# A two-layer attention and Fourier kernel on one core: a table of leans for the order of the queues, constant products in TensorE's planned gaps, and places held for the last two block groups

## The chip, the cores and the metric

The kernel runs on one core of one Trainium2 chip. The metric is device time in microseconds (us); lower is better. TensorE is called PE in the profile (its weight loads PEld), VectorE DVE, ScalarE ACT, GpSimd POOL, and SyncE SP; SP issues the DMAs.

## The reference

The input x is 2048 rows by 512. Two kinds of layer alternate, twice each; every one adds its result to x, and every one begins with a normalization of the rows.

```python
def _A_ref(x, wq, wk, wv, wo, beta):        # attention with a memory
    H = 32; Dh = D // H; N = 4; L = S // N  # 32 heads of 16, 4 segments of 512 rows
    ...
    for s in range(N):
        qs, ks, vs = q[:, :, s], k[:, :, s], v[:, :, s]
        logits = jnp.einsum("bhqd,bhkd->bhqk", qs, ks) * scale + mask
        p = _softmax(logits, axis=-1)
        a_dot = jnp.einsum("bhqk,bhkd->bhqd", p, vs)
        pq = phi(qs)
        ...                                 # a_mem = phi(q) M / (phi(q) z)
        o = g * a_mem + (1.0 - g) * a_dot
        outs.append(o)
        pk = phi(ks)
        M = M + jnp.einsum("bhld,bhle->bhde", pk, vs)
        z = z + jnp.einsum("bhld->bhd", pk)
    ...
    return o @ wo

def _B_ref(x, ...):                         # Fourier mixing, the real part
    a = jnp.einsum("bsd,ed->bse", x, dft_hid_re)
    b = jnp.einsum("bsd,ed->bse", x, dft_hid_im)
    y = jnp.einsum("ts,bse->bte", dft_seq_re, a) - jnp.einsum("ts,bse->bte", dft_seq_im, b)
    return y

x = x + _A_ref(_layernorm(x), ...)
x = x + _B_ref(_layernorm(x), ...)
x = x + _A_ref(_layernorm(x), ...)
x = x + _B_ref(_layernorm(x), ...)
```

## The kernel before

**Tiling.** The program treats an attention and a Fourier part together as one layer, so it has two. The 2048 rows are 16 row tiles of 128, four to a segment. The 32 heads are four groups of eight. Layers, segments and groups together make 32 rounds. Most large products are made in float16 with each operand split into a high and a low half; three products (high by high, high by low, low by high) are summed.

**The work of a round.** The four row tiles of a segment are loaded and normalized (`t_ln`, line 554: statistics on DVE, a power on POOL, two activations on ACT, the low half on DVE or POOL, then a transposing DMA into the tile `g`). PE makes queries and keys (`s_p`), then values (`s_v`; ACT evicts them in `t_v`, line 703). The scores are made twice: once by rows, to get each row's maximum on DVE (`s_x`, `t_max`), and once transposed (`s_st`, line 889) for the exponentials on ACT and the causal mask on POOL (`t_sel`). The masked exponentials multiply the values (`s_av`, line 912), four heads beside each other in 32 columns of the array each. The result is merged with the memory part (`s_mem`, `s_m`).

**The Fourier part.** When a segment's four groups are done, `s_o` (line 971) makes the output projection, adds x, normalizes again, and `s_ab` multiplies by the transform along the row (512). The transform along the 2048 rows is split by block groups of row tiles: `CHUNKS = [2] * 6 + [4]`, six groups of two and a last one of four. For each group and each of 16 output tiles, `s_f` (line 1120) adds the group's share; these are the long runs of `w,w` products, 3072 in all. Their results are added to `y` (`t_y`, line 1106), and with the last group `t_y` writes the finished tile. The sequence matrix comes from memory in pieces of 256 KB (`s_r`, line 1018): in layer 0 raw, to be scaled and split by `s_c` and `t_c` (a maximum on DVE, one product with ones on PE, two activations on ACT, a subtraction) and stored; in layer 1 the stored halves are read back.

**Who sets the order.** Each engine works through its instructions in the order in which the program writes them. A planner (class `Plan`, line 47) sets that order while the program is written. Every kind of work is a Python generator: a stream (`s_...`, listed in line 1154) or a task that a stream starts (`t_...`). A generator yields what its next step needs: an engine, the tiles that it reads, the places that it takes. For every candidate `Plan.ready` and the free times of the engines give the time at which the step could start, and the earliest is written next (lines 1199 and 1200):

```python
best = min(ready, key=lambda q: (q[0] - LEAN.get(q[1][2] + q[1][0][0][0], 0),
                                 PRIO.get(q[1][2] + q[1][0][0][0], 5)))
```

The key of the table `LEAN` is the generator's name and the letter of the engine (T for TensorE, V, A, G for GpSimd, Y for SyncE): `t_yY` is the write of a finished `y` tile. A positive lean makes a step look earlier by that many ns. In this kernel the table is empty (line 32).

The attention-by-value products alternate between two units, each at half of the product's cost `c` (line 159).

**Places.** One pool `w` of 50 places (`NW`, line 25) holds most working tiles. Each kind has a floor and a ceiling: `slots_free` (line 88) refuses a place that would leave another kind short of its floor. `ab` is the kind of the inputs of the transform along the rows; its ceiling is 12, and `s_f` sets its floor when it comes to a block group (lines 1126 and 1127): 12 at the last but one (two tiles of two halves and four more tiles), 8 at the last, 4 at the others. The tile kind `dft` stands for a place in the accumulator memory.

Of the kernel before, what the change touches and what calls it, by code (L numbers as in the profile page):

```python
# [1 line left out]

# [24 lines left out]
CHUNKS = [2] * 6 + [4]  # L27
# [1 line left out]
BF16 = mybir.dt.bfloat16  # L29
NEG = -1e30  # L30
TICK = 10240 / 3
LEAN = {}
APART = dict(pj=(1, 4), av=(1, 2), dft=(0, 2), sx=(2, 4), st=(2, 4), ss=(0, 4))
SHARED = dict(pj=(1, 4), av=(0, 2), dft=(1, 2), sx=(0, 2), st=(0, 2), ss=(2, 6))
HOLD, SWITCH = 700.0, 95.0
# [3 lines left out]
BATCH = 4  # L39
AFTER = 4  # L40
PRIO = {}
DEEP = 1500.0
AHEAD = 2
NR = 2
# [2 lines left out]
class Plan:  # L47
# [4 lines left out]
    def __init__(self):  # L52
        self.free = dict.fromkeys("VGATYD", 0.0)
        self.acc = {}
        self.cols = {}
        self.wr = {}
        self.rd = {}
        self.area, self.count, self.slot = {}, {}, {}
        self.fresh = set()
        self.fine = {}  # L60
        self.by = {}
        self.dma = None
        self.lands = []
        self.ports = []
        self.mode, self.units, self.begun, self.entered = "m", {}, 0.0, 0.0

    def turn(self, mode):

# [75 lines left out]
    def op(self, eng, name, args, kw):  # L144
        aps = [a for a in list(args) + list(kw.values()) if isinstance(a, bass.AP)]
        out, ins = [aps[0]], aps[1:]
        if name == "tensor_tensor_reduce":
            out.append(ins.pop())
        n = max(a.free_size() for a in aps)
        lat = self.LAT[eng]  # L150
        src = any(a.space == bass.MemoryType.PSUM for a in ins)
        if eng == "T":
            n, w = out[0].free_size(), aps[1]
            slow = 4 if w.dtype == F32 else 1
            c = max(n / 2.4 * slow, (380 if n < 32 else 200) if slow > 1 else 55) + (18 if w.dtype == F32R else 3)
            cols = n * slow * w.partition_size() / 128
            mode, unit = "m", 0
            if name == "matmul" and out[0].partition_size() == 32:
                mode, unit, c = "v", out[0].start_partition() // 32 % 2, c / 2
            elif w.partition_size() <= 64:  # L160
                mode, unit = "h", w.start_partition() // 64
                if slow > 1:
                    unit, c = 0, c / 2
        elif eng == "A":
            c = n / 1.2 + (52 if src else 93) + (93 if any(a.free_size() == 1 for a in ins) else 0)
        elif eng == "V":
            c = 68 + n / 0.96
            if name == "reciprocal":
                c = 68 + n * 6.25
            elif name == "scalar_tensor_tensor" and out[0].dtype == F32:  # L170
                c += 60
            elif name == "tensor_copy" and out[0].dtype == F16:
                c = 68 + n / 1.92
            elif name == "tensor_scalar" and out[0].dtype == F32:
                c = 68 + n / (0.87 if src else 1.32)
        elif eng == "G":
            c = 127 + n * 0.915 if name == "affine_select" else 96 + n * 2.1
            if name == "tensor_tensor" and kw.get("op") == OP.pow:
                c = 300 + n * 165
            elif name == "partition_all_reduce":  # L180
                c = 370
        else:
            stored = out[0].space == bass.MemoryType.DRAM
            c, took, tail = self.dma or ((415, 917, 364) if stored else (470, 829, 755))
            took *= out[0].nbytes() / 262144 if self.dma is None else 1
            if kw.get("transpose"):
                c, took, tail = 1325, 850, 300
        t = self.free[eng]
        for a in ins:
            t = max(t, self.wr.get(self.key(a), 0.0))  # L190
        for o in out:
            m = self.key(o)
            t = max(t, self.rd.get(m, 0.0))
            if eng == "V" and "reduce" not in name or self.by.get(m, eng) != eng:
                t = max(t, self.wr.get(m, 0.0))
        psum = [self.key(a) for a in aps if a.space == bass.MemoryType.PSUM]
        for m in psum:
            for o, u in self.acc.get(m, {}).items():
                if o != eng:
                    t = max(t, u)  # L200
        if eng == "V" and name in SHAREPORT and not src:
            for b, e in self.ports[-8:]:
                if b <= t < e:
                    t = e
        if eng == "Y" and len(self.lands) >= 8:
            t = max(t, self.lands[-8])
        if eng == "T":
            if mode == self.mode:
                t = max(t, self.begun + 7, self.units.get(unit, 0.0))
            else:  # L210
                t = max(t, max(self.units.values(), default=0.0) + SWITCH)
                self.mode, self.units, self.entered = mode, {}, t
            k = int(t / TICK)
            if self.cols.get(k - 1, 0) < 3060:
                c = min(2 * c, max(c, (k + 1) * TICK - t + c / 2))
            self.cols[int((t + c) / TICK)] = self.cols.get(int((t + c) / TICK), 0) + cols
        e = t + c
        self.free[eng] = e
        if eng == "G" and name == "tensor_tensor":
            self.ports.append((t, e))  # L220
        if eng == "T":
            self.begun = t
            self.units[unit] = e
            if len(self.units) < dict(m=1, h=2, v=2)[mode]:
                self.free[eng] = t + 7
            else:
                self.free[eng] = min(self.units.values())
        if eng == "Y":
            self.free["D"] = max(self.free["D"], e + 590) + took
            e = self.free["D"] + tail  # L230
            self.lands.append(e)
        e += lat
        for m in psum:
            self.acc.setdefault(m, {})[eng] = e
        for a in ins:
            m = self.key(a)
            self.rd[m] = max(e, self.rd.get(m, 0.0))
        for o in out:
            m = self.key(o)
            self.wr[m] = e  # L240
            self.by[m] = eng
            self.fresh.discard(m)
        for a in ins + out:
            if a.tensor.name in self.slot:
                ar, b = self.slot[a.tensor.name]
                ar["last"][b] = max(ar["last"][b], e)
# [18 lines left out]
def body(ctx: ExitStack, tc: tile.TileContext, x, wq, wk, wv, wo, beta, wd, cs, out):  # L265
    nc = tc.nc
    pl = Plan()
# [852 lines left out]
    def s_f():  # L1120
        u = 0
        held, left = {}, {}
        for j, t in units:
            layer, r = chunks[j]
            if j not in held:
                low = 2 * sum(len(chunks[j + k][1]) for k in range(2) if j % len(CHUNKS) + k == last - 1 + k)
                pl.area["ab"]["kinds"]["ab"] = low or 2 * max(len(c[1]) for c in chunks[j:j + 2]), 12
                keys = [(layer, gt, e) for gt in r for e in range(2)]
                yield gate(*[("ab", *k) for k in keys])
                held[j], left[j] = [abs_.pop(k) for k in keys], NT  # L1130
            ab = held[j]
            n = len(r) // 2
            yield gate(*[("c", u + i) for i in range(n)])
            cc = prep[u:u + n]
            u += n
            yield need("T", *cc, *ab, tag="dft")
            p = ps("dft")
            for k in range(4 * n):
                c, b = cc[k // 4], ab[k]
                sl = slice(128 * (k % 4), 128 * (k % 4) + 128)  # L1140
                for i, (x, z) in enumerate(((0, 0), (0, 1), (1, 0))):
                    T.matmul(p, c[:, x, sl], b[:, z], start=(k == 0 and i == 0), stop=(k == 4 * n - 1 and i == 2))
                if k % 4 == 3:
                    pl.close(c)
                if k < 4 * n - 1:
                    yield need("T")
            f = place[j % len(CHUNKS), t]
            spawn(t_y(p, layer, t, fyu[:, f:f + 1], j % len(CHUNKS) == last))
            left[j] -= 1
            if not left[j]:  # L1150
                pl.close(*ab)
            yield need("T")
# [2 lines left out]
        s_ld, s_r, s_c, s_m, s_av, s_st, s_o, s_ln, s_w, s_x, s_mem, s_v, s_p, s_ab, s_f, s_wo, s_k)]  # L1155
    for s in streams:
        s[0] = next(s[1])
    def settle(s):
        while callable(s[0]) and s[0]():
            s[0] = next(s[1], None)  # L1160
        return s[0] is not None and not callable(s[0])

    while streams or tasks:
# [37 lines left out]
        if best is None:  # L1201
            assert not streams and not tasks, "stuck"
            break
        best[1][0] = next(best[1][1], None)

# [43 lines left out]
```

## Time and profile before

| | |
|---|---|
| Median of 3 runs | 1746.74 us (1741.66 to 1747.06) |
| The profiled execution, its own time | 1747.35 us |
| Its span, first to last instruction | 1745.6 us |
| Instructions | 32094, of which 10998 matmuls |
| Busy: PE, DVE, ACT, POOL | 1674.4, 1094.4, 870.9, 746.2 us |
| Mean granted TensorE clock | 0.971 |
| DMA | 225.00 MB, all working transfers on SP's queue |

All instructions go through one helper, line 258, so groups are told apart by tile names and not by lines: `b` is a place in the accumulator memory, `w` one of the 50 places, `g` the transposed normalized rows, `x` and `y` the rows of x between layers and the running sum of the transform. "out<-in" names what an instruction writes and reads. A stage is a stretch of the span; a busy time is given in us of that stretch. The granted clock of a stretch is a mean over its time: 1.00 is full speed.

### The profile page before, as it was taken

What the parts mean: (1) busy time and instruction counts of PE and PEld (TensorE: products, weight loads), DVE (VectorE), ACT (ScalarE), POOL (GpSimd) and SP (SyncE); (2) the same over time, 40 slices, a digit from 0 to 9 for tenths busy, and PEclk for the clock granted to TensorE, in tenths of its full rate; (3) what the DMA queues carried; (4) which work ended last, traced back from release to release, by engine and by line L of the source; (5) the groups of instructions that cost most, each with busy time, mean ns of one, the idle gap of its engine ahead of it and who ended that gap; (6) DMA issues with size and microseconds to landing.
All of it is one profiled execution on the core that took longest, in us unless ns stands there. A gap on an engine that the chain in (4) does not pass through costs nothing.

```text
span 1745.6 us, 32094 instructions
## 1 busy us (share of the span) xinstructions
PE 1674.4 (96%) x10998; PEld 730.6 (42%) x10998; DVE 1094.4 (63%) x3525; ACT 870.9 (50%) x1481; POOL 746.2 (43%) x1284
## 2 busy tenths in 40 slices
PE   6888899998999999999999999999999999999999
PEld 3333344443344443444535344443444443344444
DVE  7885856787675967654578676566675856443221
ACT  5597467555548365644366755464446334412000
POOL 4466355555546264633244644444535334312000
PEclk9788999999999999999989999999999999999999
DMA  8537445554247443334845654354444342131423
GB/s 194 165 102 205 109 113 156 150 145 128 77 125 212 139 130 107 108 105 135 223 139 189 188 164 121 74 138 132 113 120 122 94 110 85 56 121 23 136 85 118
DMA packets 217076, 225.00 MB, mean 129 GB/s; under 512 B 112968, under 2 KB 135496, under 8 KB 216912
## 3 DMA queue, kind: packets, MB, share of 16 engines
q1 hardware_dynamic: 216912, 222.95, 45.6%
q8 instruction: 86, 1.41, 0.3%
q14 instruction: 78, 0.64, 0.1%
HBM read 137.40 MB, written 61.87 MB: 114 GB/s over the span
## 4 chain that ended last, share of the span: by engine, by line
PE 80%; DVE 7%; issue 4%; DMA 3%; ACT 3%; POOL 2%; SPq 1%; DVEq 0%; POOLq 0%; ACTq 0%
PE b L258 80%; DVE junk L258 3%; ACT w L258 3%; POOL w L258 2%; DMA w<-w 1%; SPq L258 1%; DVE w L258 1%; DVE y L258 1%; DVE mx L258 1%; DMA x<-y 0%; DMA w<-in_x_dram 0%; DMA y<-in_wv_dram 0%; DVE bst L258 0%; DMA w<-x 0%; DVE cgm L258 0%
## 5 line engine op out<-in xcount | busy, mean ns | idle before, releaser
L258 PEld LDWEIGHTS <-w 128*128 128x128 f16 x4992 | 466.2, 98 | 636.9 <-issue 121.5
L258 PE MATMUL b<-w,w 128*128 128x512 f16 x3072 | 709.9, 381 | 4.2 <-POOL w L258 1.4
L258 ACT ACTIVATE w<-b,fac 128x512 f32<-128x512 f32 (+1 forms) x728 | 417.6, 653 | 196.1 <-PE b L258 191.8
L258 DVE CUSTOM_DVE_ANT_0 junk<-b,cmask 128x128 bf16<-128x128 f32 (+3 forms) x1024 | 437.1, 485 | 70.9 <-PE b L258 70.1
L258 POOL TENSOR_TENSOR w<-w,w 128x512 f16<-128x512 f32 (+1 forms) x260 | 309.2, 1193 | 239.1 <-ACT w L258 204.7
L258 POOL TENSOR_SCALAR_AFFINE_SELECT w<-w 128x128 f32<-128x128 f32 (+2 forms) x704 | 236.7, 348 | 272.6 <-ACT w L258 268.1
L258 DVE SCALAR_TENSOR_TENSOR y<-b,fyu,y 128x512 f32<-128x512 f32 x200 | 149.1, 745 | 210.7 <-PE b L258 209.8
L258 PE MATMUL b<-g,w 128*128 128x512 f16 x768 | 191.1, 394 | 6.7 <-POOL w L258 3.0
L258 ACT ACTIVATE w<-w,csc 128x512 f16<-128x512 f32 (+1 forms) x256 | 179.5, 721 | 25.2 <-DVE csc L258 20.3
L258 PE MATMUL b<-w,vt 128*32 128x512 f32 (+3 forms) x2048 | 181.5, 469 | 6.9 <-POOL w L258 4.7
L258 PE MATMUL b<-wd,w 128*128 128x512 f16 x768 | 182.1, 385 | 4.6 <-DMA w<-w 4.3
L258 ACT ACTIVATE w<-b 128x512 f16<-128x512 f32 x128 | 76.4, 599 | 218.0 <-PE b L258 210.6
L258 DVE SCALAR_TENSOR_TENSOR w<-b,w 128x512 f16<-128x512 f32 x128 | 87.9, 688 | 150.2 <-ACT w L258 149.2
L258 PE MATMUL b<-kst,qst 48*128 48x128 f16 (+3 forms) x1024 | 125.0, 309 | 10.9 <-DVE mx L258 5.0
L258 PE MATMUL b<-qst,kst 50*128 50x512 f16 (+3 forms) x1024 | 119.5, 308 | 10.4 <-DVE mx L258 3.8
L258 ACT ACTIVATE w<-w 128x512 f16<-128x512 f32 (+1 forms) x144 | 90.6, 632 | 58.1 <-DVE w L258 55.9
L258 PEld LDWEIGHTS b<-w,vt 128*32 128x32 f32 x2048 | 56.7, 113 | 95.8 <-issue 52.2
L258 PE MATMUL b<-w,g 128*128 128x128 f16 x1536 | 94.4, 219 | 0.4 <-ACT w L258 0.2
L258 PEld LDWEIGHTS <-g 128*128 128x128 f16 x1536 | 87.8, 98 | 13.9 <-issue 9.1
L258 DVE STREAM_TRANSPOSE w<-b 128x512 f32<-128x512 f32 x112 | 76.4, 699 | 22.1 <-PE b L258 13.7
L258 PE MATMUL b<-wo,w 128*128 128x512 f16 x384 | 89.3, 381 | 0.0
L258 PEld LDWEIGHTS <-kst 50*128 50x128 f16 x1024 | 37.5, 95 | 120.8 <-issue 109.5
(99 smaller groups left out, 1017.8 us busy)
## 6 DMA issues: line engine op xcount, KB each, us to landing
w<-in_cs_dram SPq DMA_DIRECT2D x128, 256.0 KB, 3.6
cc<-w SPq DMA_DIRECT2D x128, 256.0 KB, 2.5
w<-cc SPq DMA_DIRECT2D x128, 256.0 KB, 3.3
w<-w SPq DMA_DIRECT2D x96, 256.0 KB, 3.2
d<-w SPq DMA_DIRECT2D x128, 128.0 KB, 2.5
w<-in_x_dram SPq DMA_DIRECT2D x32, 256.0 KB, 3.2
qst<-d SPq DMA_DIRECT2D x64, 128.0 KB, 3.2
kst<-d SPq DMA_DIRECT2D x64, 128.0 KB, 2.8
```

The source lines that it names most:

```text
L258: r = f(*args, **kw)
```

## The change

It has four parts.

1. **Leans.** The table `LEAN` gets eight entries: transposed scores on PE 150 ns earlier, loads of the sequence matrix 600 ns earlier, the activations of the first normalization 1500 ns earlier, writes of `y` 2000 ns later, loads of x for the output projection 300 ns earlier, the scaling work of the sequence matrix 150 ns later, loads of x for the first normalization 1000 ns later, evictions of values 1000 ns earlier.
2. **Constant products.** `Plan` also records PE's work as (begin, end, columns); `lately(t)` is the number of columns worked in the 3413 ns before t. Ahead of each step on PE that the planner writes, `t_warm` looks at the planned gap. If the mask constant exists ("CM"), the gap less 300 ns is at least 500 ns, fewer than 4200 columns were worked lately, and an accumulator place of the kind `dft` is free by then, it writes products of the constant `onesb` by itself, 512 columns each, until the gap is full or 4200 columns are reached. Nothing reads the result.
3. **Cost of attention by value.** The planner's cost on a unit goes from `c / 2` to `c / 2 + 12` ns.
4. **Places.** The floor of `ab` is 12 at the last two block groups of a layer; before, it was 12 at the last but one and 8 at the last.

```diff
-LEAN = {}
+LEAN = dict(s_stT=150.0, s_rY=600.0, t_lnA=1500.0, t_yY=-2000.0, s_oY=300.0, s_cV=-150.0, s_lnY=-1000.0, t_vA=1000.0)
...
+WARM, IDLE, SPARE = 4200, 500.0, 300.0
...
+    def lately(self, t):
+
+        return sum(c * max(0.0, min(e, t) - max(b, t - TICK)) / (e - b) for b, e, c in self.work)
...
-                mode, unit, c = "v", out[0].start_partition() // 32 % 2, c / 2
+                mode, unit, c = "v", out[0].start_partition() // 32 % 2, c / 2 + 12
...
+            self.work.append((t, t + c, cols))
+            while self.work[0][1] < t - 3 * TICK:
+                self.work.popleft()
...
-                low = 2 * sum(len(chunks[j + k][1]) for k in range(2) if j % len(CHUNKS) + k == last - 1 + k)
-                pl.area["ab"]["kinds"]["ab"] = low or 2 * max(len(c[1]) for c in chunks[j:j + 2]), 12
+                low = 2 * max(len(c[1]) for c in chunks[j:j + 2])
+                if j % len(CHUNKS) >= last - 1:
+                    low = 2 * sum(CHUNKS[last - 1:])
+                pl.area["ab"]["kinds"]["ab"] = low, 12
...
+    def t_warm(at):
+        at -= SPARE
+        if "CM" not in done or at - pl.free["T"] < IDLE or pl.lately(at) >= WARM:
+            return
+        r = pl.slots_free(("dft",))
+        if r is None or r > at - IDLE:
+            return
+        old = {b: (pl.area["dft"]["last"][b], pl.area["dft"]["kind"].get(b)) for b in range(8)}
+        p = ps("dft")
+        ar, b = pl.slot[p.tensor.name]
+        n = 0
+        while max(pl.free["T"], r) + 220 < at and pl.lately(at) < WARM:
+            T.matmul(p, onesb, onesb.unsqueeze(1).to_broadcast([128, 4, 128]), start=True, stop=True)
+            n += 1
+        pl.close(p)
+        pl.wr[p.tensor.name] = pl.rd[p.tensor.name] = ar["last"][b] = old[b][0]
+        pl.acc.pop(p.tensor.name, None)
...
+        if best[1][0][0] == "T":
+            t_warm(best[0])
         best[1][0] = next(best[1][1], None)
```

More of the change, by code (lines that the diff above doesn't have):

```diff
@@ L1 @@
+from collections import deque
 from contextlib import ExitStack
@@ L64, in __init__ @@
         self.ports = []
+        self.work = deque()
         self.mode, self.units, self.begun, self.entered = "m", {}, 0.0, 0.0
+    def lately(self, t):
+        return sum(c * max(0.0, min(e, t) - max(b, t - TICK)) / (e - b) for b, e, c in self.work)
     def turn(self, mode):
```

## The prediction

> **What bounds the kernel now.** I read the page first, for the busy shares, the strip of 40 slices and the chain that ended last; then the cores, for the mean granted clock; then busy time by stage.
>
> ```profile
> span 1745.6 us, 32094 instructions
> PE 1674.4 (96%) x10998; PEld 730.6 (42%) x10998; DVE 1094.4 (63%) x3525; ACT 870.9 (50%) x1481; POOL 746.2 (43%) x1284
> ...
> PEclk9788999999999999999989999999999999999999
> ...
> PE 80%; DVE 7%; issue 4%; DMA 3%; ACT 3%; POOL 2%; SPq 1%; DVEq 0%; POOLq 0%; ACTq 0%
> ```
> ```profile
> core 0: 1745.6 us, clock 0.971
> ```
> ```profile
> 0.00:208.00 208.00, 165.75 (x1149) 73.25 (x1150) 156.40 (x583) 132.85 (x222) 105.73 (x177) 0.85 0.60 159
> 208.00:800.00 592.00, 579.92 (x3835) 248.01 (x3833) 409.73 (x1262) 349.27 (x591) 305.59 (x503) 0.98 0.45 127
> 800.00:900.00 100.00, 92.72 (x511) 42.02 (x509) 59.17 (x199) 45.52 (x72) 37.31 (x45) 0.91 0.68 188
> 900.00:1445.00 545.00, 539.59 (x3915) 236.95 (x3913) 368.84 (x1275) 289.83 (x504) 246.12 (x463) 1.00 0.48 129
> 1445.00:1745.60 300.60, 296.41 (x1594) 130.39 (x1594) 100.25 (x215) 53.40 (x93) 51.45 (x98) 1.00 0.29 91
> ```
>
> In the stage rows the columns are length, PE, PEld, DVE, ACT, POOL, granted clock, DMA share, GB/s. TensorE is the bound: no other engine is above 63%, and 80% of the chain is PE. What an order of work can win is PE's idle time and the time at a lower clock. Idle is 1745.6 - 1674.4 = 71.2 us: 42.25 in the first 208 us (208 - 165.75), 12.1 to 800, 7.3 at the change of layer (800 to 900), 5.4 to 1445, 4.2 after. The clock costs at most (1 - 0.971) x 1745.6 = 50.6 us: 31.2 in the first stretch (0.15 x 208), 11.8 in the second (0.02 x 592), 9.0 in the third (0.09 x 100), nothing that shows later. So the last 845 us hold under 10 us in all, and a gain comes from the first 900 us or not at all. In the first 208 us DVE is busy 156.40 and ACT 132.85: there PE often waits for them, and a higher clock alone shortens less than its 31.2.
>
> **Part by part: the constant products.** The planner now puts products of `onesb` by itself into TensorE's queue wherever it plans a gap of 800 ns or more (IDLE + SPARE) with less than 4200 columns in the last 3.41 us. Nobody reads them. Their use is the clock, so I set PE's gaps beside the granted clock right behind them. PE's timeline, with the idle time before a piece in brackets, and the price of a 512-column product:
>
> ```profile
> 55.22 0.61 PE L258 MATMUL b<-g,w 128*128 128x512 f16 x1 [3.01 <-POOL w L258]
> 190.56 1.46 PE L258 MATMUL b<-wd,w 128*128 128x512 f16 x3 [4.32 <-DMA w<-w]
> 418.92 0.37 PE L258 MATMUL b<-identf,mx 128*32 128x128 f32 x1 [1.10 <-DVE mx L258]
> 562.77 1.92 PE L258 MATMUL b<-w,vt 128*32 128x256 f32 x12 [2.09 <-POOL w L258]
> 820.88 0.17 PE L258 MATMUL b<-cam,onesb 128*128 128x4 bf16 x1 [0.70 <-DVE cam L258]
> 822.46 0.61 PE L258 MATMUL b<-w,w 128*128 128x512 f16 x2 [0.75 <-ACT w L258]
> 824.45 11.79 PE L258 MATMUL b<-w,w 128*128 128x512 f16 x46 [1.38 <-POOL w L258]
> 838.32 4.02 PE L258 MATMUL b<-g,w 128*128 128x512 f16 x10 [2.08 <-DMA g<-w]
> 964.46 3.23 PE L258 MATMUL b<-w,vt 128*32 128x512 f32 x16 [1.03 <-DVE mv L258]
> 1689.77 51.75 PE L258 MATMUL b<-w,w 128*128 128x512 f16 x239
> ```
> ```profile
> 190.00:197.00 7.00, 6.44 (x17) 1.71 (x18) 4.84 (x18) 1.44 (x2) 2.43 (x3) 0.51 0.32 67
> 418.80:422.20 3.40, 3.28 (x20) 1.13 (x21) 0.86 (x2) 2.21 (x5) 3.01 (x5) 0.50 0.78 193
> 562.20:565.60 3.40, 2.83 (x15) 0.85 (x15) 1.29 (x2) 3.37 (x7) 2.10 (x5) 0.50 0.60 120
> 838.60:842.00 3.40, 3.40 (x10) 1.25 (x9) 0.00 (x0) 0.00 (x0) 0.00 (x0) 0.51 0.00 0
> 965.00:968.30 3.30, 3.30 (x18) 0.66 (x11) 3.27 (x13) 2.25 (x4) 2.07 (x2) 0.50 0.21 79
> 681.60:685.00 3.40, 2.58 (x11) 0.60 (x10) 3.33 (x13) 3.40 (x7) 1.17 (x4) 1.00 0.51 158
> 685.00:692.00 7.00, 6.76 (x28) 1.30 (x29) 7.00 (x24) 2.45 (x5) 2.46 (x7) 0.51 0.00 0
> ```
>
> Behind five of these gaps (4.32, 1.10, 2.09, 2.08, 1.03) a stretch at half clock follows with 6.44, 3.28, 2.83, 3.40 and 3.30 us of PE work. At full clock that work takes half, so the five are worth (6.44 + 3.28 + 2.83 + 3.40 + 3.30) / 2 = 9.6 us. All lie in stretches where PE is the bound afterwards, so the saving reaches the end. The gap of 3.01 at 52 us I count at nothing, because PE waits for others all round it. I take -8: a gap that the planner doesn't foresee gets no product. The ends: the seven gaps of 0.8 us and over in the fence are 15.0 us, at 51.75 / 239 = 0.217 us per product 69 products; if all of them stood where PE turns out to have work, +15. If they lift the clock of the whole first stretch too and PE bounds it, -9.6 - 31.2 = -41. The last two rows are a limit on the part: between 681.6 and 685 PE is idle 0.82 us in all, in pieces, and the clock still halves for 7 us. Products that need a gap of 0.8 us don't reach that.
>
> The Trainium skill ("TensorE: Matmul & The Clock Gate", section "Why this matters for your kernels") says to avoid PE gaps of more than about 3 us, since one idle window brings the half clock back. By that rule products in gaps of 1 to 2 us would bring nothing, and the part would be worth the 3.2 us behind the gap of 4.32 alone (1730 in the sum below). The trace disagrees: the clock halved behind gaps of 1.03, 1.10 and 2.09 us.
>
> **The leans at the change of layer.** A lean moves a step in the choice by so many ns; positive goes earlier. Writes of `y` go 2.0 us later (t_yY), loads of x for the next normalization 1.0 us later (s_lnY), loads of the sequence matrix 0.6 us earlier (s_rY); all three stand in SP's one queue. The chain there, and what SP waited for between 800 and 842 us:
>
> ```profile
> 806.11 4.30 DMA x<-y
> ...
> 811.78 3.45 DMA x<-y
> ...
> 816.14 3.97 DMA w<-in_cs_dram
> 820.14 0.70 DVE cam L258
> ...
> 834.38 3.90 DMA g<-w
> ```
> ```profile
> SPq L258 <- DMA x<-y: 9.6, 4, 3.9
> ```
>
> SP stood 9.6 us on x loads whose rows were still being written, and a matrix load behind one of them came at 816.14; its maximum, scaling and split are the waits of 0.70, 0.75 and 1.38 us in the PE rows. Letting matrix loads pass removes up to 2.8 us of PE idle. Against it, write and load of x, at up to 3.0 us later, feed the normalization whose transposed tile lands at 838, where PE waits 2.08 us. So: -2.8 for the matrix loads, +0.8 for the x rows, since PE still has transform work beside most of that delay; I take -2. Ends: -4.9 (0.70 + 0.75 + 1.38 + 2.08, all gone) to +3.0.
>
> **The other leans.** t_lnA and t_vA put the normalization's and the values' activations up to 1.5 and 1.0 us earlier in ACT's queue; s_stT, s_oY and s_cV are ties of 0.15 to 0.3 us.
>
> ```profile
> L258 ACT ACTIVATE w<-w,mv,rs 128x512 f32<-128x512 f32 x56 | 45.5, 812 | 51.2 <-DVE mv L258 51.0
> L258 ACT ACTIVATE w<-w 128x512 f16<-128x512 f32 x96 | 60.6, 632 | 29.9 <-DVE w L258 27.8
> L258 ACT ACTIVATE vt<-b 128x512 f32<-128x512 f32 x32 | 19.1, 596 | 46.5 <-PE b L258 46.5
> L258 PE MATMUL b<-w,vt 128*32 128x512 f32 x512 | 70.8, 674 | 2.0 <-DVE mv L258 1.3 <-ACT w L258 0.6 <-DVE y L258 0.2
> ```
>
> No instruction is added, so the sum is what idle and low clock they can take away: in 208 to 800 and 900 to 1445, 12.1 + 5.4 + 11.8 = 29.3 us. Taking off what the products already get there ((3.28 + 2.83 + 3.30) / 2 = 4.7) leaves 24.6; I take a third, -8, because earlier inputs (normalized rows, values) bring segments to PE sooner, while each lean also holds something back. In the first 208 us I take a tenth of the idle, -4, since loads and DVE set the pace. Ends: -24.6 - 14.1 (a third of 42.25) and, upwards, the slower rival below.
>
> **The two that I cost at nothing.** The plan's price of an attention-by-value product goes from c / 2 to c / 2 + 12 on each of two units: 32 rounds x 4 key tiles x 8 heads = 1024 products x 6 ns = 6 us of plan time over the whole kernel, against 70.8 us that the chip spends on the widest form alone (two instructions per product). It moves orders only; 0, at most 6 either way. The floor for DFT inputs at the last block group rises from 8 to 12 places of 50. Its cover: PE is idle 4.2 of the last 300.6 us. At the end of layer 0 four places are kept from other kinds for some 60 us; if that makes a matrix load late, it costs what the load at 816 cost, 2.8 us. I take 0.
>
> **Sum.** -8 - 2 - 8 - 4 = -22 us from 1747.35 us, the profiled execution's own time (1.75 above its span, 0.61 above the median shown): 1725.35, on the median's scale 1724.7. I forecast 1725, with its own range 1712 to 1740. A measurement of this kernel tells about 0.3% from no change, 5.2 us.
>
> **Rivals.**
> *The waits only change places.* After 208 us PE is already busy 1508.6 of 1537.6 us; a new order has new gaps of the same size, and the products help only behind the longest gap, 3.2 us: 1744. For it: the waits are many and small, spread over POOL, DVE, ACT and DMA. Against it: the matrix load behind a waiting queue is a place, not chance. Chance 0.13. By the Trainium skill's rule above, that on gaps of about 3 us, the products would do just this.
>
> *ACT is held for the normalization: slower.* ACT takes its queue in the order written: a normalization put 1.5 us early makes ACT stand until its mean and scale arrive, with exponentials of the attention behind it, then POOL's masks, then PE's products by the values. Place: the starts of segments 2 to 8, four row tiles each. Price: half the lean, 0.75 us, per tile, and one half-clock window per segment (3.40 us of work, 1.7 lost): 7 x (4 x 0.75 + 1.7) = 32.9, less the 22: 1758. It decides from five of the seven segments on (5 x 4.7 = 23.5). For it: ACT already stood 51.0 us for `mv` in the row above. Against it: ACT has half its span free, and PE mostly has other products to run. Chance 0.17.
>
> *A larger gain.* Half of the idle and clock loss from 208 to 1445 ((24.8 + 20.8) / 2 = 22.8) and a third of both in the first stretch ((42.25 + 31.2) / 3 = 24.5) go: 47 us, 1700. For it: most of the loss is in one stretch, with clock and idle feeding each other. Against: DVE at 156.40 of 208 us. Chance 0.18.
>
> *The products don't appear,* because no place for a transform's sum is free in time: the forecast without its 8, 1733; it lies in the forecast's own range.
>
> **The numbers.** Forecast 0.52, larger gain 0.18: faster 0.70. Same 0.13, slower 0.17. The range goes from 1693, which takes in most of the larger gain, to 1758, the slower rival's own value; about half of that rival and a part of the larger gain stay outside.
>
> **What would show it.** Right: a group of `onesb` products, some 60 to 150, most of them in the first 210 us and around 800 to 900; granted clock above 0.85 in the first stretch and 1.00 behind gaps now filled; PE idle from 208 to 1445 down from 24.8 to about 15 us; matrix loads no longer behind x loads. Wrong: idle in the first 208 us still 42 us with a higher clock (then the clock wasn't on the path there); ACT's idle for `mv` above 62 us in all with PE waiting for POOL's masks at segment starts (the slower rival); products standing where PE's input had landed.

## The result, and the profile after

The changed kernel takes 1700.53 us (median; 1698.0 to 1702.07), the kernel before 1746.9 us beside it: a ratio of 0.9735, 95% interval 0.9717 to 0.9754. It is faster by 46 us. The forecast was 22 us, so the sign was right and the size was half. The time is that of the prediction's rival with the larger gain.

The page of the changed kernel and its cores, then its busy time by the stages that the prediction used (length, PE, PEld, DVE, ACT, POOL, granted clock, DMA share, GB/s):

```profile
span 1698.9 us, 32303 instructions
PE 1660.4 (98%) x11103; PEld 726.9 (43%) x11103; DVE 1087.5 (64%) x3525; ACT 871.1 (51%) x1481; POOL 746.3 (44%) x1284
...
PEclk9979999999999999999999999999999999999999
```
```profile
core 0: 1698.9 us, clock 0.993
```
```profile
0.00:208.00 208.00, 187.35 (x1321) 83.52 (x1321) 161.56 (x601) 135.26 (x227) 110.60 (x182) 0.95 0.62 166
208.00:800.00 592.00, 586.49 (x3935) 253.28 (x3932) 419.98 (x1291) 369.71 (x619) 322.04 (x519) 1.00 0.49 139
800.00:900.00 100.00, 98.45 (x691) 46.25 (x689) 70.48 (x251) 54.15 (x92) 42.42 (x65) 1.00 0.67 193
900.00:1445.00 545.00, 537.98 (x3954) 232.26 (x3953) 362.90 (x1262) 285.70 (x502) 242.63 (x478) 1.00 0.46 123
1445.00:1698.90 253.90, 250.12 (x1213) 111.61 (x1211) 72.60 (x121) 26.24 (x44) 28.58 (x42) 1.00 0.27 86
```

The granted clock is 1.00 behind 208 us and 0.95 ahead of it; half-clock loss of at most 50.6 us has become 11.9 (0.007 x 1698.9). PE is idle 38.5 us in all, where it was 71.2. The products, by form, and where they stand on PE's timeline (the first and the last three of 20 pieces):

```profile
L268 PE MATMUL b<-onesb 128*128 128x512 bf16 x105 | 28.9, 413 | 2.5 <-DVE onesb L268 1.7 <-DVE mx L268 0.8
```
```profile
1.73 6.95 PE L268 MATMUL b<-onesb 128*128 128x512 bf16 x18 [1.73 <-DVE onesb L268]
...
850.19 0.59 PE L268 MATMUL b<-onesb 128*128 128x512 bf16 x2 [0.43 <-DVE mx L268]
851.58 1.02 PE L268 MATMUL b<-onesb 128*128 128x512 bf16 x4 [0.37 <-DVE mx L268]
853.07 0.39 PE L268 MATMUL b<-onesb 128*128 128x512 bf16 x1
```

Of the 105, 98 stand in the first 192 us and 7 at 850 us. Idle time and products together are 38.5 + 28.9 = 67.4 us, hardly under the 71.2 of idle before; what fell is the time of the real work, from 1674.4 to 1660.4 - 28.9 = 1631.5 us, a fall of 42.9 us, near the 38.7 by which the clock loss fell (50.6 - 11.9). It would be easy to end here and say that the products keep the clock up and that this is the gain. But there are none between 192 and 850 us, and there the half-clock stretches went too. The question for the experiments was therefore what made the gain: the order, by what each lean means (theory A), the products on the chip (B), or a new order as such, whatever the leans mean (C, later sharpened to D)?

### The profile page after: what moved, and what is told of

Its sections match the earlier page's. It is cut to its first block, busy times and chain, and to the rows that moved or that the text cites. A ratio compares the mean times of both kernels' runs of the same rounds, so it can differ in the third digit from the quotient of the medians.

```text
span 1698.9 us, 32303 instructions
## 1 busy us (share of the span) xinstructions
PE 1660.4 (98%) x11103; PEld 726.9 (43%) x11103; DVE 1087.5 (64%) x3525; ACT 871.1 (51%) x1481; POOL 746.3 (44%) x1284
## 4 chain that ended last, share of the span: by engine, by line
PE 79%; DVE 7%; ACT 4%; issue 4%; DMA 3%; POOL 1%; SPq 1%; DVEq 0%; ACTq 0%; POOLq 0%
PE b L268 79%; ACT w L268 4%; DVE junk L268 3%; DMA w<-w 2%; DVE w L268 1%; POOL w L268 1%; DVE mx L268 1%; SPq L268 1%; DMA w<-x 1%; DVE y L268 0%; DMA w<-in_cs_dram 0%; DVE bst L268 0%; DMA w<-in_x_dram 0%; DMA g<-w 0%; DVE amax L268 0%
## 5 line engine op out<-in xcount | busy, mean ns | idle before, releaser
L268 PE MATMUL b<-g,w 128*128 128x512 f16 x768 | 180.8, 379 | 1.6 <-DMA g<-w 0.9
L268 PE MATMUL b<-wd,w 128*128 128x512 f16 x768 | 177.7, 379 | 1.0 <-DMA w<-w 0.7
L268 PE MATMUL b<-kst,qst 48*128 48x128 f16 (+3 forms) x1024 | 115.0, 302 | 3.8 <-DVE mx L268 1.2
L268 DVE DVE_READ_ACCUMULATOR2_ANT mx<- 128x1 f32 x1024 | 85.4, 83 | 0.0
```

What stands on the lines that cost most here:

```text
L268: r = f(*args, **kw)
```

## The experiments

Every number is a median of timed runs beside the kernel before on the same chip. "Plan" is no measurement: it is the landing of the last output as the planner itself reckons it while it writes the program, against the same number of the kernel before. Theory D and the leans of the later runs go by it.

| Kernel | us | before beside it | ratio, 95% interval | us against before | plan against before's plan |
|---|---|---|---|---|---|
| changed | 1700.5 | 1746.9 | 0.9735 (0.9717 to 0.9754) | -46.4 | -26.3 |
| e1 products only | 1727.9 | 1743.3 | 0.9923 (0.9893 to 0.9953) | -15.4 | -7.1 |
| e2 leans only | 1734.7 | 1743.3 | 0.9945 (0.9924 to 0.9965) | -8.6 | -4.2 |
| e3 changed, no products | 1772.5 | 1743.3 | 1.0173 (1.0151 to 1.0194) | +29.2 | +38.1 |
| e6 leans x 0.9 | 1715.4 | 1744.4 | 0.9830 (0.9809 to 0.9851) | -29.0 | -15.6 |
| e7 changed, without +12 | 1731.3 | 1744.4 | 0.9922 (0.9902 to 0.9942) | -13.1 | -2.1 |
| e8 changed, old places | 1716.8 | 1744.4 | 0.9842 (0.9817 to 0.9867) | -27.6 | -17.8 |
| e9 near leans, early plan | 1699.3 | 1742.4 | 0.9750 (0.9735 to 0.9764) | -43.2 | -29.4 |
| e10 near leans, late plan | 1754.8 | 1742.4 | 1.0071 (1.0055 to 1.0087) | +12.4 | +19.7 |
| e11 +12 only | 1726.7 | 1742.4 | 0.9909 (0.9894 to 0.9924) | -15.7 | -5.0 |
| e12 no products, plan always warm | 1729.2 | 1742.4 | 0.9923 (0.9906 to 0.9939) | -13.3 | -10.2 |
| e13 no products, early plan | 1712.4 | 1747.7 | 0.9804 (0.9760 to 0.9847) | -35.4 | -19.6 |
| e14 leans only, early plan | 1719.8 | 1747.7 | 0.9846 (0.9800 to 0.9891) | -28.0 | -19.3 |

### One part at a time: e1, e2, e3

e1 is the kernel before with `t_warm` and `lately` alone; e2 has the eight leans alone; e3 is the changed kernel without the call of `t_warm`:

```diff
-        if best[1][0][0] == "T":
-            t_warm(best[0])
```

> Constant products alone on the kernel before: no leans, old cost of the attention-by-value product, old places. Theory A (order: the leans make the larger part, because 98 of the 105 products of the changed kernel stand in the first 192 us while two thirds of the gain, 31 of 46 us, appear after 208 us): 1728 to 1738 us, and the half-clock stretches between 400 and 900 us are still there. Theory B (clock: the products make nearly all of it, and what is won early carries on): 1700 to 1710 us.

> The eight leans alone on the kernel before. Theory A (order): 1712 to 1722 us, clock in the first 208 us still near 0.85, from 208 to 900 us near 1.00. Theory B (products): 1738 to 1750 us. Theory C (no meaning in the leans: any change of order redraws the gaps): anywhere between 1720 and 1760 us, and the gains of the two parts alone don't add up to the whole.

> The changed kernel without the constant products, all else as in it; the planner orders anew without them. Theory A: 1712 to 1720 us. Theory B: 1735 us or more.

Alone, the products bring 15.4 us and the leans 8.6. Without the products, everything else makes the kernel 29.2 us slower than before. So the parts don't add: taking the products out of the changed kernel costs 72 us (1772.5 - 1700.5), putting them into the old one gains 15. No theory that gives each part a price fits this. Of the expectations, A just misses e1's time (1727.9), and the half-clock stretches that it kept from 400 to 900 us are mostly gone (granted clock 1.00 there, 0.96 in the kernel before); e2 misses A and B and falls to C; e3 fits B alone. One wait of e3 shows what such a loss looks like; PE's timeline:

```profile
503.53 5.34 PE L268 MATMUL b<-w,w 128*128 128x512 f16 x24
514.11 0.16 PE L268 MATMUL b<-cam,onesb 128*128 128x4 bf16 x1 [5.24 <-DVE cam L268]
514.21 1.46 PE L268 MATMUL b<-qst,kst 50*128 50x512 f16 x6
```

The one small product that scales the sequence matrix stands in PE's queue ahead of the scores, and its input is late on DVE. PE waits 5.24 us for 0.16 us of work. In the trace of before the wait for this input is 0.70 us (at 820.88, in the prediction's rows); the new order made this one.

### The products at a fixed order: e4, e5, e15 to e18

To price the products on the chip, the order must not move. e4 (run again as e18, with the changed kernel as e17 on the same chip) plans them but doesn't write them, so every other instruction stands as in the changed kernel:

```diff
-            T.matmul(p, onesb, onesb.unsqueeze(1).to_broadcast([128, 4, 128]), start=True, stop=True)
+            pl.op("T", "matmul", (p, onesb, onesb.unsqueeze(1).to_broadcast([128, 4, 128])), {})
```

e5 is the reverse: the kernel before in its own order, with products written into the gaps of its own plan, which doesn't count them. e15 and e16 take the products off e9 and e10.

```diff
+            nc.tensor.matmul(p, onesb, onesb.unsqueeze(1).to_broadcast([128, 4, 128]), start=True, stop=True)
...
-            T.matmul(p, onesb, onesb.unsqueeze(1).to_broadcast([128, 4, 128]), start=True, stop=True)
```

> The changed kernel, planned with the constant products, so that every other instruction stands in the order of the changed kernel, but the products themselves aren't written. This is the clock effect of the products by itself at one order. If the products act through the clock: half-clock time in the first 208 us returns to some 50 us (clock near 0.85) and 12 to 20 us are lost, 1712 to 1720 us. If they act through the plan alone (they only changed the order): 1698 to 1704 us.

> The kernel before, every instruction in its old order, with constant products written into the gaps that its own plan shows (same thresholds), and the plan left as if they weren't there. This measures the term of the prediction for the products, -8 us, at the old order. If the clock behind the gaps counts as worked out there: 1733 to 1740 us, half-clock time down from 103 to under 80 us. If a product in a gap is worth as little as in the changed kernel (5 us between it and the kernel with the products planned but not written): 1739 to 1744 us.

> The kernel of the near, early leans (1699 us), planned with the products, the products not written. As at the change's order (5 us): 1702 to 1708 us. If the products' clock counts fully, by the half-clock time that they avoid: 1710 us or more.

> The kernel of the near, late leans (1755 us), planned with the products, the products not written. There 53.7 us of PE's time went to products, more than in the other runs, so many stand where PE had work. If a misplaced product costs its time and the clock behind it is worth as much: 1750 to 1760 us. If the products cost more than they bring there: 1735 to 1750 us.

> The changed kernel itself, beside the next run on the same chip: 1698 to 1704 us, ratio to the kernel before 0.972 to 0.976.

> The changed kernel's order without its products once more, beside the changed kernel on the same chip. If the products' clock is worth what the times of the two earlier runs say: 4 to 6 us above the changed kernel. By their ratios to the kernel before: 9 to 12 us above it. If it is nothing, as at the old order: within 2 us of it.

| Order | without products | with | products are worth |
|---|---|---|---|
| changed (e18, e17, one chip) | 1706.6 | 1700.6 | 6.0 us |
| changed (e4, and the first measurement) | 1705.7, ratio 0.9796 (0.9773 to 0.9818) | 1700.5, ratio 0.9735 | 5 to 11 us |
| e9 (e15) | 1704.5, ratio 0.9762 (0.9724 to 0.9801) | 1699.3, ratio 0.9750 | 2 to 5 us |
| e10 (e16) | 1757.9, ratio 1.0067 (1.0045 to 1.0089) | 1754.8, ratio 1.0071 | nothing to 3 us |
| before (e5), ratio 1.0019 (1.0004 to 1.0033) | 1744.4 | 1747.4 | -3.0 us |

Where the two stand beside different chips, the range is from the difference of the times to that of the ratios. e4 lies between its two expectations, nearer to that in which the products act through the plan.

e15 and e16 lie in their first ranges, e17 and e18 in theirs (4 to 6 us). e5 missed both of its ranges: the products save nothing at the old order. (The 53.7 us of products that e16's expectation names for e10 are 56.3 us in e10's trace.)

So of the changed kernel's 44 us beside e17 (1744.7 - 1700.6), about 6 are the products on the chip and 38 the order, in which the products count as planned work. The 6 is rough: the means of e17 and e18 lie 4.7 us apart, with some 3 us either way. Now the page and the cores of e18, which has no products, and the products of e17 with its busy time:

```profile
PE 1646.0 (97%) x10998; PEld 719.9 (42%) x10998; DVE 1085.7 (64%) x3525; ACT 871.0 (51%) x1481; POOL 746.6 (44%) x1284
```
```profile
core 0: 1704.6 us, clock 0.987
```
```profile
PE 1661.0 (98%) x11103; PEld 726.8 (43%) x11103; DVE 1087.2 (64%) x3525; ACT 871.0 (51%) x1481; POOL 746.2 (44%) x1284
L268 PE MATMUL b<-onesb 128*128 128x512 bf16 x105 | 27.7, 398 | 2.5 <-DVE onesb L268 1.7 <-DVE mx L268 0.8
```

Span is PE's busy time plus its idle time, so the pages split the gain. From the kernel before to e18 the span falls by 41.0 us: PE's idle time from 71.2 to 58.6 us, by 12.6, and its busy time for the same 10998 matmuls from 1674.4 to 1646.0 us, by 28.4. The half-clock loss (as above, one less the clock, times the span) falls by as much, from 50.6 to 22.2 us. So the order by itself, without one constant product on the chip, brings most of the higher clock. From e18 to e17 (span 1698.2 us) idle time falls by another 21.4 us and the real work by 12.7 (1646.0 to 1661.0 - 27.7 = 1633.3), against 27.7 us of products.

At the old order they bring nothing, although they do to the clock what the prediction said in the stretches where they stand. The kernel before and e5, the same two stretches (columns as above):

```profile
137.00:149.10 12.10, 8.94 (x39) 2.48 (x31) 8.39 (x20) 11.91 (x20) 8.93 (x17) 0.50 0.75 237
186.00:197.00 11.00, 6.68 (x21) 1.71 (x18) 8.66 (x28) 2.88 (x4) 4.23 (x5) 0.69 0.44 107
```
```profile
137.00:149.10 12.10, 11.88 (x59) 4.58 (x55) 7.32 (x15) 11.89 (x20) 9.02 (x16) 1.00 0.81 231
186.00:197.00 11.00, 10.83 (x51) 4.50 (x48) 5.93 (x20) 2.88 (x4) 3.88 (x4) 1.00 0.34 82
```

The clock goes from 0.50 and 0.69 to 1.00. Now PE's timeline of e5 in these stretches (its products are issued directly and bear line 1187):

```profile
137.03 2.33 PE L1187 MATMUL b<-onesb 128*128 128x512 bf16 x10
139.41 0.61 PE L268 MATMUL b<-qst,kst 50*128 50x512 f16 x4
139.96 1.68 PE L1187 MATMUL b<-onesb 128*128 128x512 bf16 x7
141.69 0.39 PE L268 MATMUL b<-qst,kst 50*128 50x512 f16 x2
142.02 1.90 PE L1187 MATMUL b<-onesb 128*128 128x512 bf16 x8
143.98 0.39 PE L268 MATMUL b<-qst,kst 50*128 50x512 f16 x2
144.30 1.69 PE L1187 MATMUL b<-onesb 128*128 128x512 bf16 x7
146.04 1.46 PE L268 MATMUL b<-g,w 128*128 128x512 f16 x6
...
147.74 1.46 PE L268 MATMUL b<-g,w 128*128 128x512 f16 x6
149.12 1.06 PE L268 MATMUL b<-w,vt 128*32 128x512 f32 x8
...
185.45 2.76 PE L1187 MATMUL b<-onesb 128*128 128x512 bf16 x12
188.27 0.34 PE L268 MATMUL b<-kst,qst 48*128 48x384 f16 x2
188.54 3.41 PE L1187 MATMUL b<-onesb 128*128 128x512 bf16 x15
192.01 0.34 PE L268 MATMUL b<-kst,qst 48*128 48x384 f16 x2
192.28 4.06 PE L1187 MATMUL b<-onesb 128*128 128x512 bf16 x18
196.40 0.81 PE L268 MATMUL b<-wd,w 128*128 128x512 f16 x3
...
563.73 1.91 PE L1187 MATMUL b<-onesb 128*128 128x512 bf16 x5 [1.56 <-ACT w L268]
```

and of the kernel before, the same instructions:

```profile
140.22 2.39 PE L258 MATMUL b<-qst,kst 50*128 50x512 f16 x8 [2.46 <-DMA qst<-mhl]
143.32 2.74 PE L258 MATMUL b<-g,w 128*128 128x512 f16 x6 [0.70 <-DMA w<-w]
...
146.47 2.72 PE L258 MATMUL b<-g,w 128*128 128x512 f16 x6
149.12 1.06 PE L258 MATMUL b<-w,vt 128*32 128x512 f32 x8
...
185.57 0.66 PE L258 MATMUL b<-kst,qst 48*128 48x384 f16 x6
190.56 1.46 PE L258 MATMUL b<-wd,w 128*128 128x512 f16 x3 [4.32 <-DMA w<-w]
```

The product by the values starts at 149.12 in both, and in both PE comes to it straight from the work ahead of it. So the equal start is a tie: of the 12.1 us, PE was idle 3.2 before and worked 8.9 at half clock; in e5 the same work takes 4.3 us (11.88 - 7.60), and the 32 products take 7.60 (2.33 + 1.68 + 1.90 + 1.69), the idle time and what the clock gave. The plan saw gaps between the scores; on the chip the eight scores ran without a break from 140.22 on, and the only gaps were 2.46 us ahead of them and 0.70 behind. In e5, 22 of the products stand between and behind scores, and the `g,w` products start at 146.04 instead of 143.32. At 186 us it is the same: the plan saw three gaps between pairs of scores, where the chip has only one, behind them, and the 45 products (12 + 15 + 18) push the transform from 190.56 to 196.40, 5.8 us late.

Over the whole kernel e5's products took 44.7 us. PE's idle time fell by 21.7, from 71.2 to 49.5 (span 1743.8 less 1694.3 busy), and its real work by 24.8, from 1674.4 to 1649.6 (1694.3 - 44.7). So 23.0 us of products lie beyond the idle time that they filled, and they took back nearly all that the real work had gained. The two profiled executions end 1.8 us apart, e5 ahead; that it is 3.0 behind rests on the medians, and no gain is what both say.

### The edits costed at nothing: e6, e7, e8, e11

e6 multiplies each lean by 0.9. e7 takes the 12 ns out of the changed kernel, e8 its places; e11 has the 12 ns alone on the kernel before:

```diff
-                mode, unit, c = "v", out[0].start_partition() // 32 % 2, c / 2
+                mode, unit, c = "v", out[0].start_partition() // 32 % 2, c / 2 + 12
```

> The changed kernel with every lean at nine tenths. Theory A (the leans mean something: matrix loads before x loads, normalization first): a tenth less of each moves hardly anything, 1698 to 1708 us. Theory C (one good draw among many orders): the order is drawn anew, 1710 to 1760 us.

> The changed kernel without the 12 ns on the planner's cost of an attention-by-value product. The prediction costed this part at nothing. Theory A: 1696 to 1706 us. Theory C: 1710 to 1760 us, although no instruction is added or taken away.

> The changed kernel with the old floors of the input places at the last block group (8 for 12). The prediction costed this part at nothing. The order up to the last block group of layer 0, near 700 us, should be the same as in the changed kernel whatever the theory, so at most what comes after can move. Theory A: 1697 to 1704 us. Theory C: up to 15 us either way, all of it after 700 us.

> The 12 ns on the planner's cost of an attention-by-value product, alone, on the kernel before. Theory A: nothing, 1740 to 1748 us. Theory D: its plan ends 5 us earlier than that of the kernel before, so 1733 to 1742 us.

None of these edits adds or removes an instruction of the computation. With the order the planner also sets which of DVE and POOL takes a few of them (DVE 3525 instructions before and 3523 in e11, POOL 1284 and 1286), and how many constant products it writes (126, 155 and 135 in e6, e7 and e8; 105 in the changed kernel). A tenth off the leans costs 15 us, taking out the 12 ns 31, the old places 16. In e8 the output projection of the fourth segment, the last of layer 0, starts 0.9 us later than in the changed kernel and that of the fifth 10.9 us later, so the loss does come behind the last block groups, as expected, and is just over the 15 us expected. e6 and e7 fall in the range of C and outside that of A. The 12 ns alone gain 15.7 us on the kernel before, a third of the whole gain, with nothing else. My expectation for e11, nothing or 2 to 9 us, was missed to the good side. So, with e6, the leans are no set of corrections each worth something; any nudge of the planner writes another program.

### A draw that the plan sees: e9, e10, e12, e13, e14

By then the last column of the table stood beside the times, and theory D was formed: the choice in line 1199 of the kernel before is greedy, so that each nudge deals the order anew; the plan's own end says how good the deal is; and the leans of the change are one good deal. Two sets of leans near the change's, with the same signs, were picked for an early and a late plan.

```diff
-LEAN = dict(s_stT=150.0, s_rY=600.0, t_lnA=1500.0, t_yY=-2000.0, s_oY=300.0, s_cV=-150.0, s_lnY=-1000.0, t_vA=1000.0)
+LEAN = dict(s_stT=172.0, s_rY=636.0, t_lnA=1558.0, t_yY=-1999.0, s_oY=359.0, s_cV=-167.0, s_lnY=-885.0, t_vA=1120.0)  # e9
+LEAN = dict(s_stT=82.0, s_rY=754.0, t_lnA=1352.0, t_yY=-2032.0, s_oY=274.0, s_cV=-115.0, s_lnY=-885.0, t_vA=846.0)   # e10
```

e12 has no products and a planner without the doubled cost (`if self.cols.get(k - 1, 0) < 3060:` becomes `if False:`). e13 is e3 and e14 is e2 with leans for an early plan.

> The changed kernel with other leans of the same signs, each within a fifth of the change's (matrix loads 636, normalization 1558, y writes -1999, x loads -885 and 359, scores 172, scaling -167, values 1120 ns), chosen among many because the planner's own last landing comes earliest, 3 us before that of the changed kernel. Theory A (the leans have a meaning of their own): 1698 to 1704 us. Theory D (a draw that the plan sees: the chip follows the plan's own end, whatever the leans say): 1694 to 1701 us. The two hardly differ here; the next run parts them.

> The changed kernel with leans of the same signs and near the change's sizes (matrix loads 754, normalization 1352, y writes -2032, x loads -885 and 274, scores 82, scaling -115, values 846 ns), whose plan ends 46 us later than that of the changed kernel. Theory A: under 1712 us, since every step leans the same way by about as much. Theory D: 1740 to 1755 us, no gain left over the kernel before.

> The changed kernel without constant products, in plan or on the chip, and with a planner that never doubles PE's cost after a window of few columns. Theory E (what the products do is to keep the plan's clock full, so that the plan orders for a fast PE): near the kernel with the products planned but not written, 1702 to 1712 us. Theory D: its plan ends 16 us later than the changed kernel's, so 1715 to 1725 us. Theory B (products on the chip): 1735 us or more.

> The changed kernel without constant products, in plan or on the chip, as in the run that took 1772 us, with leans of the same signs near the change's (matrix loads 576, normalization 1449, y writes -2093, x loads -1074 and 275, scores 237, scaling -97, values 1037 ns) whose plan ends earliest among many: 58 us before that run's plan. Theory D: the chip follows, 1709 to 1722 us. If products are needed (Theory B): 1735 us or more.

> The kernel before with leans alone, as in the run of the change's leans alone (1735 us), with other sizes (matrix loads 672, normalization 1424, y writes -1737, x loads -759 and 396, scores 95, scaling -140, values 808 ns) whose plan ends 15 us earlier than that run's. Theory D: 1712 to 1725 us. Theory A (the leans' meaning): 1730 to 1738 us as before.

e9 and e10 part the theories. Both lean every step the same way by similar amounts and both have the products; one is as fast as the changed kernel, the other 12.4 us slower than the kernel before. Busy time by stage of e10, and its products:

```profile
208.00:800.00 592.00, 583.12 (x3855) 254.00 (x3854) 397.94 (x1232) 346.39 (x583) 304.65 (x490) 0.99 0.45 130
900.00:1445.00 545.00, 534.59 (x3867) 233.82 (x3866) 354.48 (x1241) 287.86 (x500) 239.25 (x462) 0.99 0.45 124
```
```profile
L268 PE MATMUL b<-onesb 128*128 128x512 bf16 x197 | 56.3, 424 | 3.9 <-DVE mx L268 1.8 <-DVE onesb L268 1.7 <-ACT w L268 0.2
```

Its PE looks as busy as that of the changed kernel (97% and 98%), and its clock from 208 us on is nearly as full. But 56.3 us of its busy time are products, twice as much; idle time is 49.9 us against 38.5, and the mean clock 0.983 against 0.993: the order has more waits, and the products fill only a part of them. Without products on the chip (e16, 1675.8 us busy of a span of 1757.5) that order lies 52.9 us behind e18's, 23.1 of it idle time and 29.8 busy time for the same 10998 matmuls, at a clock of 0.970 against 0.987. With e13 and e14 the other half is shown: without any product on the chip or in the plan, other leans reach 1712.4 where the change's leans gave 1772.5, and 1719.8 on the old kernel where they gave 1734.7. e12 was to show whether the products help by keeping the plan's clock full. It took 1729.2 us, more than theory E (to 1712) and a little more than D (to 1725) expected, so that is not what the products do.

Over the 13 kernels the gain on the chip runs with the gain in the plan (the correlation of the two last columns is 0.98, and 0.95 without the two extremes, e3 and e10), and every one of them does better on the chip than in the plan, by 3 to 20 us. Theory D stands: formed after e1 to e8, its ranges held e9, e10, e13 and e14, and missed e11 by 6 us and e12 by 4. A falls with e6 and e10, B with e4, e5, e13 and e18. No run beats the changed kernel clearly: e9 is 1.2 us under it, inside both intervals.

## Why the prediction was right or wrong

**What bounds the kernel: right.** The gain came from idle and low clock in the first 900 us. Idle from 208 to 1445 went from 24.8 to 5.5 + 1.55 + 7.0 = 14.1 us (I wrote about 15), the clock to 0.95 and 1.00.

**"All lie in stretches where PE is the bound afterwards, so the saving reaches the end. I take -8": wrong.** At the old order, for which it was worked out, the products save nothing (the median is 3.0 us longer); at the new one they save about 6. The failing step is to let the products stand in the chip's gaps and cost nothing there: only 1.6 us (9.6 to 8) were taken off because the planner might not see a gap. The plan's gaps are not the chip's. Of the five gaps that were priced, e5 has products at two (45 ahead of the transform once at 190.56, and 5 at 563.73), and none within 5 us of 418.92, 838.32 and 964.46; 146 of its 168 stand in the first 208 us. The 45 cost 5.8 us where I credited 3.2. Over the whole kernel the real work did get shorter, by 24.8 us, more than I counted; the products took 23.0 us beyond the idle time. The sign that I had named, products standing where PE's input had landed, is what came. The count in the changed kernel (105, most of them ahead of 210 us) was right. The Trainium skill's advice ("TensorE: Matmul & The Clock Gate", "Why this matters for your kernels") on gaps over 3 us was set against the traces there. The time of e5 can't test it, since the products beyond the gaps took back what the clock gave; the clock speaks against it, as it halved behind gaps of 1.03 to 2.09 us in the trace of before.

**The leans, -2 - 8 - 4 = -14: the number near, the step wrong.** The leans alone gave -8.6, and that this is near is luck: other leans of the same signs, alone too, gave -28.0 (e14). Leans, 12 ns and places together, without the products, gave +29, and near leans in the full change gave -43 and +12. The step that fails is to read each lean as moving one wait by its own size. At the change of layer what I described did happen: SP's wait for rows being written fell from 9.6 us (800 to 842 us) to 5.3, in a wider window (760 to 860 us, as the change of layer is earlier; in that window before has 9.6 too):

```profile
SPq L268 <- DMA x<-y: 5.3, 3, 2.7
```

and PE's idle from 800 to 900 us from 7.3 to 1.55. That the leans did this, and not the new order as a whole, no run shows.

**"It moves orders only; 0, at most 6 either way", and 0 for the places: wrong.** The 12 ns alone are worth 15.7 us, and 31 in company; the places 16 in company. I bounded an edit of the order by the size of its parameter. The bound of such an edit is the spread of orders, and by the runs here that is from 1699 to 1772 us. This is the mis-step that matters most, because it holds for the leans as well: with it, the sum of parts is not a sum. That products, leans and 12 ns measured alone come to 39.7 us (15.4 + 8.6 + 15.7) of the 46.4 is no support for adding: leans and 12 ns are 24.3 of it, and together with the places they lost 29.2 (e3). What the runs show in place of the three small terms (-14 for the leans, 0 and 0) is a new order of some 38 us, 41.0 by the pages: 12.6 less idle time and 28.4 less busy time.

**The rivals.** ACT held for the normalization didn't come: its wait for `mv` is 39.1 us, where it was 51.0.

```profile
L268 ACT ACTIVATE w<-w,mv,rs 128x512 f32<-128x512 f32 x56 | 45.4, 810 | 39.3 <-DVE mv L268 39.1
```

"The waits only change places" is what the products do at the old order (e5) and what the leans do in e10, but not what the change did. "A larger gain" named 1700 us with half of the idle and clock loss after 208 us gone and a third ahead of it. The time is right and the shares were too small: idle and clock loss together fell from 121.8 to 50.4 us (71.2 + 50.6 to 38.5 + 11.9), and 28.9 us of that went to the products. Its reason, clock and idle feeding each other, fits e18 and e16, where both move together with the order alone, but no run parts the two.

**What stays open.** Which waits of the order make up the 38 us was not taken apart, and with orders that differ all along it can hardly be done by one more edit. Nor is it shown why the kernel before lies 38.7 us above its own plan (1746.9 against 1708.2), the changed one only 18.6 (1700.5 against 1681.9) and the others from 21 to 31; of the 46 us the plan sees 26. Single leans and the places alone were not run.

## What to carry to other kernels

Where a greedy planner writes the order, treat an edit of its costs or preferences as a new deal: bound it by the spread of a few neighbouring deals, and don't add up parts measured alone. To price one mechanism, hold the order fixed and add or leave out that mechanism by itself (planned but not written, or written but not planned). Before pricing work that is to fill gaps, check that the gaps in which it will be written are those of the trace; afterwards set its time against the idle time and the real work that went (in e5, 44.7 against 21.7 and 24.8), and compare start times of the same instruction.

## What the runs showed of the hardware that was not expected

Products of ones by ones, standing between real work, raise the granted clock to 1.00 (0.50 to 1.00 from 137 to 149 us in e5, which has 32 of them there). An order can raise it without them (0.971 before, 0.987 in e18). And products beyond a gap cost their time: 45 of them, 10.2 us (2.76 + 3.41 + 4.06), over a gap of 4.32 us moved the next real start by 5.8 us.
